# Sums for x of groups 3 to 8 over all 64 features at once, with feature halves exchanged between partition quarters

## The chip, the cores and the metric

The kernel runs on one core of a Trainium2 chip. The core has five engines that run side by side, each in its own order and tied together by semaphores: PE (TensorE, matrix products into PSUM; PEld is its weight load), DVE (VectorE), ACT (ScalarE), POOL (GpSimd) and SP (SyncE, used here only to issue transfers). The metric is the device time of one execution, in microseconds (us); smaller is better.

## The reference

Two blocks follow one another. The first is an attention with a polynomial sketch in place of the softmax; the second is a feed-forward block with an ELU.

```
q, k, v: (4, 4, 1088, 32) float32        S1, S2: (8, 32)
w_in: (128, 2048)      w_out: (2048, 128)

phi(x) = outer product of (S1 x) and (S2 x), 64 features for each row
kv  = sum over s of phi(k)[s, f] * v[s, d]          (64 x 32 for each batch and head)
z   = sum over s of phi(k)[s, f]
x   = (phi(q) @ kv) / (phi(q) . z + 1e-6)           heads side by side: (4352, 128)
h   = x @ w_in
out = where(h > 0, h, exp(min(h, 0)) - 1) @ w_out   (4352, 128)
```

The sums of the title are `phi(q) @ kv`: for each query row and head, 64 features against a 64 x 32 matrix.

## The kernel before

**Tiling.** The 4352 rows of x are 68 half tiles of 64 rows, made into nine groups of eight (the last has four). The feed-forward block goes through the groups in steps `(g, cp)`, each for one of eight pairs of 128-wide slices of the 2048: `mm1` (first product, line L256), the ELU on ACT and DVE (L827, L829, L835), and two steps later the second product (`mm2`, or for most groups `mm2_seven`, L756, with sums made ahead on POOL). There are 64 steps for groups 0 to 7 and a loop for the last group.

**Where x comes from.** While the steps of earlier groups run, x of later groups is prepared. `extra` is a table written out by hand: `at(n, ...)` puts a piece of work right after `mm1` of step n, `mid` after the first half of its ELU, `late` after the second half. All engines keep the order in which the program emits; nothing is reordered by a scheduler.

For one of the groups 2, 3, 4 (with 5), 6 (with 7) and 8:
- `queries(...)` holds PE's part. `q1` (L544) multiplies the queries by S1, S2 and the z-weighted sketch, for the group that comes next; `q5` (L661) makes the sums of the group at hand. Both write to the same four PSUM banks, two of which are those of the next step's `mm1`.
- `q2_den`, `q2_a`, `q2_half` make `phi(q) / denominator` (tile `qp`): 128 partitions, i.e. four quarters of 32 query rows, with the 64 features along the free axis.
- `q4` (L651) is one DVE transpose in 32x32 blocks: in each quarter of the partitions, 32 features come onto the partitions and 32 query rows onto the free axis, for both halves f of the 64 features one after the other (tile `qpT`).
- `q5` then takes, for each head r and each quarter w, two 32x32 matmuls, one for each feature half f; the second adds onto the first. The 16 of f = 0 come first, then `q1`, then the 16 of f = 1.
- `q5_out` (L672) copies the result to `xg`, the operand of `mm1`.

Step 15 holds the queries call for group 2, step 22 for group 3, 30 for groups 4 and 5, 46 for 6 and 7, 62 for 8. The transposes `q4` stand late in steps 14 (`at`), 20, 27 and 28 (two halves), 37 and 38, and 60.

**The sums of K^T V.** `KT_out(b)` transposes the sums of batch b on DVE (L441), writes them to DRAM (`kvd`, L442) and reads them back into each of the four partition quarters (`kvs`, L445; batch 0 into one quarter only). Groups 2 and 3 use batch 1, groups 4 and 5 batch 2, 6 and 7 batch 3; group 8 has rows of all four.

**Transfers.** Nearly all are issued by SP, in program order: the loads, `kvd` and `kvs`, and the output rows (L804 in `fin_seven_b`, 16 transfers for a group; L861 in `fin1`, 8). Each has one of eight semaphores in turn and waits for the transfer eight before it.

Of the kernel before, what the change touches and what calls it, by code (L numbers as in the profile page):

```python
# [12 lines left out]
F32 = mybir.dt.float32  # L13
# [14 lines left out]
def kernel(  # L28
# [21 lines left out]
    nc = tc.nc  # L50
    B, H, S, D = q.shape
    R = S1.shape[0]
    P = 128
# [10 lines left out]
    const = ctx.enter_context(tc.tile_pool(name="const", bufs=1))  # L64
    work = ctx.enter_context(tc.tile_pool(name="wk", bufs=2))
# [75 lines left out]
    wide = S1.dtype != F32  # L141
# [17 lines left out]
    if wide:  # L159
        raw_2 = const.tile([P, 2, 4 * P, 2], U32, name="raw")  # L160
# [163 lines left out]


    kvS = const.tile([P, H, D], F32, name="kvS")
    kvs = {b: const.tile([P, H, 2, D], F32, name=f"kvs{b}") for b in range(B)}
    dram = ctx.enter_context(tc.tile_pool(name="dram", bufs=1, space=bass.MemoryType.DRAM))
    kvd = {b: dram.tile([P, 2 * D], F32, name=f"kvd{b}")[:] for b in range(B)}
    kv_ps, feats, wzs, kf_ps = {}, {}, {}, []  # L330
# [107 lines left out]
    def KT_out(b):  # L438

        kt = work.tile([P, 2 * D], F32, name="kvt", tag="kvt")  # L440
        nc.vector.transpose(kt[:], kv_ps[b][:, :R * R])  # L441
        nc.sync.dma_start(kvd[b], kt[:])  # L442
        src = kvd[b].rearrange("(h p) x -> p h x", h=H)
        for w in range(4 if b else 1):
            nc.sync.dma_start(kvs[b][32 * w:32 * w + 32].rearrange("p h f d -> p h (f d)"), src)  # L445

    def ZC(b, ps):
        zl = work.tile([P, H * R], F32, name="zl", tag="zl")
        nc.scalar.copy(zl[:], ps[:, R * R:R * R + H * R])
        return zl  # L450
# [30 lines left out]
    abw, ans, qp, qpT, xg, xps = {}, {}, {}, {}, {}, {}  # L481
# [48 lines left out]
    def quarter_of(g, w):  # L530

        n = un[g] // 2
        return (*half_tile(g + n * w // 8, n * w % 8), n)

    def q1(g, ps, o, opened):
        for w in range(4):
            b, t, n = quarter_of(g, w)
            m, qs = 64 * n, qE[:, b:b + 1, :] if g == NQ - 1 and b < 2 else qT[b][:, t:t + n, :]
            qs = qs.rearrange("p t s -> p (t s)")
            if g == 2:  # L540
                m, qs = 2 * m, _ap(qs, [[8 * 64, 2], [1, m]])
            for r in range(4):
                rows = slice(32 * r, 32 * r + 32)
                nc.tensor.matmul(ps[r][32 * w:32 * w + 32, o:o + m], SWs[rows, b].rearrange("p x r -> p (x r)"),  # L544
                                 qs[rows], start=not opened, stop=True, skip_group_check=True,
                                 tile_position=(32 * r, 32 * w))
        abw[g] = ps, o
# [79 lines left out]
            nc.scalar.copy(to[:, w], xp[w][:, :256].rearrange("p (m s) -> p m s", s=P))  # L627


    def heads(g):  # L630
        return 2 if un[g] > 4 else H

    def q2_a(g, i):
        m = heads(g) * un[g]
        p = psum.tile([P, 512], F32, name="qa", tag="aux")
        ans[g, i] = p[:, :m * R].rearrange("p (m r) -> p m r", r=R)
        nc.scalar.copy(p[:, :m * R], ans[g][:, m * i:m * i + m].rearrange("p m r -> p (m r)"))

    def q2_half(g, i):
        m = heads(g) * un[g]  # L640
        r = slice(m * i, m * i + m)
        qp[g, i] = work.tile([P, 4 * H, R, R], F32, name="qp", tag="qp", bufs=2)
        a_, b_ = ans.pop((g, i)) if (g, i) in ans else ans[g][:, r], abw[g][:, r, :R]
        nc.vector.tensor_mul(qp[g, i][:, :m], _ap(a_, list(a_.ap[1:]) + [[0, R]]),
                             _ap(b_, [b_.ap[1], [0, R], b_.ap[2]]))

    def q4(g, i=0):

        m = heads(g) * un[g]
        qpT[g, i] = work.tile([P, 4 * H, 2, 32], F32, name="qpT", tag="qpT", bufs=2)  # L650
        nc.vector.transpose(qpT[g, i][:, :m].rearrange("p m f s -> p (m f s)"),  # L651
                            qp.pop((g, i))[:, :m].rearrange("p m i j -> p (m i j)"))

    def q5(g, ps, f):
        m4 = un[g]
        for r in range(4):
            i, o = divmod(m4 * r, heads(g) * un[g])
            for w in range(4):
                b, t, n = quarter_of(g, w)
                rows = slice(32 * w, 32 * w + 32)  # L660
                nc.tensor.matmul(ps[w][32 * r:32 * r + 32, :64 * n], kvs[b][rows, r, f, :],  # L661
                                 qpT[g, i][rows, o:o + 2 * n, f, :], start=(f == 0), stop=(f == 1),
                                 skip_group_check=True, tile_position=(32 * w, 32 * r))
        xps[g] = ps

    def q5_out(g, i=0):
# [7 lines left out]
    def queries(g5, g1, n):  # L674

        hs[steps[n]] = [psum.tile([P, 512], F32, name="h", tag="h", bufs=4) for c in range(2)]
        ps = hs[steps[n]] + [psum.tile([P, 512], F32, name="qps", tag="aux") for _ in range(2)]
        if g5 is not None:
            q5(g5, ps, 0)
        if g1 is not None:  # L680
            q1(g1, ps, 256 if g5 is not None else 0, g5 is not None)
        if g5 is not None:
            q5(g5, ps, 1)


# [297 lines left out]
    def late(n, f, *a):  # L983
        extra.setdefault((n, 1), []).append((f, *a))
# [10 lines left out]
    late(2, make_SWs)  # L995
    late(3, Z_share, 0)
    late(3, KT_out, 0)
    zls = {}

    def sums_out(b):  # L1000
        zls[b] = ZC(b, kv_ps[b])
        KT_out(b)
# [32 lines left out]
    for n, g, nx in ((12, None, 2), (15, 2, None), (22, 3, 4), (30, 4, 6), (46, 6, 8), (62, 8, None)):  # L1035
        at(n, queries, g, nx, n + 1)
        if g is not None:
            mid(n, q5_out, g)
        if nx == 2:
            at(n, weights7, slice(NP - 2, NP))  # L1040
            at(n, q1_out_two, (0, 1))
            mid(n, q1_out_two, (2, 3))
        elif nx is not None:
            mid(n, q1_out, nx)
        if g is not None and len(units[g]) > 1:
            late(n, q5_out, g, 1)
    late(12, q2_den, 2)
    late(13, q2_half, 2, 0)
    at(14, q4, 2)
    mid(15, q2_den, 3)  # L1050
    late(19, q2_a, 3, 0)
    late(19, q2_half, 3, 0)
    late(20, q4, 3)
    late(22, q2_den, 4)
    for n, g, i in ((25, 4, 0), (26, 4, 1), (32, 6, 0), (35, 6, 1)):
        late(n, q2_a, g, i)
    at(26, q2_half, 4, 0)
    late(26, q2_half, 4, 1)
    late(27, q4, 4, 0)
    late(28, q4, 4, 1)  # L1060
    late(31, q2_den, 6)
# [12 lines left out]
    for n in range(2, N):  # L1074
        g, cp = steps[n]
# [29 lines left out]
        g, cp = before  # L1105
# [10 lines left out]
    g = NQ - 2  # L1116
# [53 lines left out]
```

## Time and profile before

| | us |
|---|---|
| median of 3 runs (lowest, highest) | 262.6 (262.52, 263.65) |
| the profiled execution, in all | 262.6 |
| its span | 260.5 |
| PE busy | 255.0 (98%) |
| DVE busy | 186.8 (72%) |
| ACT busy | 183.2 (70%) |
| POOL busy | 158.9 (61%) |

The profile is one execution. Its span runs from the first to the last instruction; 2.1 us lie around it. A line of the time order gives the start in us from the span's start, the length, the engine, the line of the kernel, the operation, what it writes and reads, and a count when neighbours are merged; "SPq" is an issue on SP's queue. One matmul on float32 makes two records. "64*32" at a matmul is the piece of the array that it uses, rows by columns; "64x288" is rows by columns of the moving operand. Busy times of PE overlap, since matmuls are pipelined, so distances from start to start are the better measure.

### The profile page before, as it was taken

Reading aid. Unit: us, or ns where it says so; the run is one execution under the profiler, and the core shown is the slowest. Engines: PE = TensorE matmul, PEld = TensorE weight load, DVE = VectorE, ACT = ScalarE, POOL = GpSimd, SP = SyncE. Lnnn points to the kernel's source line nnn. Section 1 sums busy time; section 2 is a strip of 40 time slices with the busy share of each in tenths; the row PEclk is TensorE's granted clock in tenths of the full one; section 3 lists DMA queues with packets and bytes.
Section 4 is the critical chain, followed back from the end, with each engine's and each line's share of the span. In section 5 each row is a group of like instructions: output and inputs, shape, how many; then the busy total and the mean of one; then the engine's idle time right before and its main releaser. Section 6 shows DMA issues by size and latency. Waiting matters only on the chain.

```text
span 260.5 us, 9833 instructions
## 1 busy us (share of the span) xinstructions
PE 255.0 (98%) x4187; PEld 158.7 (61%) x4187; DVE 186.8 (72%) x352; ACT 183.2 (70%) x358; POOL 158.9 (61%) x202
## 2 busy tenths in 40 slices
PE   8899999999999999999999999999999999999994
PEld 7652333453346667676666666665666666668994
DVE  6899999999988958997567576743465446674641
ACT  2469878766667577776687777775877777777792
POOL 4420007002279996788678798888588888887410
PEclk9999999999999999999999999999999999999999
DMA  6998089012011210012100200020001100110012
GB/s 172 325 362 223 4 236 263 16 48 67 14 19 28 34 32 13 3 18 36 26 0 4 35 8 3 0 31 12 3 3 29 17 4 0 25 18 3 3 28 38
DMA packets 28507, 14.30 MB, mean 55 GB/s; under 512 B 21392, under 2 KB 26640, under 8 KB 28464
## 3 DMA queue, kind: packets, MB, share of 16 engines
q1 hardware_dynamic: 28032, 13.32, 21.1%
q8 instruction: 33, 0.54, 0.9%
q10 hardware_dynamic: 368, 0.30, 0.3%
q0 software_dynamic: 64, 0.07, 0.1%
q14 instruction: 10, 0.08, 0.1%
HBM read 11.31 MB, written 2.36 MB: 52 GB/s over the span
## 4 chain that ended last, share of the span: by engine, by line
PE 97%; DVE 1%; ACT 0%; issue 0%; DVEq 0%
PE h L256 45%; PE pb L756 17%; PE pa L756 13%; PE o L256 5%; PE pb L732 4%; PE ol L256 3%; PE idle L264 1%; PE kv L432 1%; PE h L661 1%; PE abp L340 1%; PE qps L661 1%; PE h L544 1%; PE qtp L614 1%; DVE qp L602 1%; PE xps L621 0%; PE kfps L362 0%
## 5 line engine op out<-in xcount | busy, mean ns | idle before, releaser
L256 PE MATMUL h<-xg,W 128*32 128x512 f32 (+3 forms) x904 | 130.8, 539 | 0.3 <-ACT xg L627 0.3
L835 DVE SCALAR_TENSOR_TENSOR gg<-e,h 128x512 f32<-128x512 f32 x128 | 86.0, 682 | 53.1 <-ACT e L829 48.7
L827 ACT ACTIVATE e<-h 128x512 f32<-128x512 f32 x128 | 75.5, 590 | 46.4 <-PE h L256 44.5
L829 ACT ACTIVATE e<-e 128x512 f32<-128x512 f32 x128 | 80.9, 632 | 3.8
L717 POOL TENSOR_TENSOR tt<-gg 128x512 f32<-128x512 f32 x50 | 64.2, 1284 | 29.5 <-DVE gg L835 23.7
L256 PEld LDWEIGHTS h<-xg,W 128*32 128x32 f32 (+1 forms) x904 | 43.0, 122 | 42.9 <-issue 34.6
L720 POOL TENSOR_TENSOR tt<-gg,tt 128x256 f32<-128x256 f32 x50 | 36.9, 739 | 3.9
L719 POOL TENSOR_TENSOR tt<-tt,gg 128x256 f32<-128x256 f32 x50 | 36.7, 735 | 3.9
L756 PEld LDWEIGHTS pa<-gg,W 128*64 128x64 f32 (+1 forms) x496 | 23.7, 126 | 22.8 <-issue 22.7
L756 PE MATMUL pa<-gg,W 128*64 128x128 f32 (+1 forms) x496 | 30.6, 274 | 0.0
L756 PE MATMUL pb<-tt,SS 128*64 128x128 f32 (+1 forms) x480 | 29.6, 273 | 0.0
L756 PEld LDWEIGHTS pb<-tt,SS 128*64 128x64 f32 (+1 forms) x480 | 22.8, 126 | 0.0
L756 PE MATMUL pa<-tt,SS 128*32 128x128 f32 (+1 forms) x288 | 21.2, 273 | 0.0
L756 PE MATMUL pb<-tt,W 128*64 128x128 f32 (+1 forms) x256 | 19.9, 273 | 0.0
L756 PE MATMUL pb<-gg,SS 128*64 128x128 f32 (+1 forms) x256 | 19.9, 273 | 0.0
L134 POOL TENSOR_TENSOR raw<-raw,tiny 128x512 f32<-128x512 f32 x1 | 1.0, 1043 | 24.7 <-DVE raw L129 24.7
L256 PE MATMUL o<-gg,W 128*32 128x512 f32 x128 | 15.3, 595 | 0.0
L756 PEld LDWEIGHTS pa<-tt,SS 128*32 128x32 f32 (+1 forms) x288 | 13.7, 124 | 0.0
L756 PEld LDWEIGHTS pb<-tt,W 128*64 128x64 f32 (+1 forms) x256 | 12.8, 125 | 0.0
L756 PEld LDWEIGHTS pb<-gg,SS 128*64 128x64 f32 (+1 forms) x256 | 12.8, 125 | 0.0
L732 PE MATMUL pb<-gg,W 128*32 128x256 f32 x192 | 11.5, 380 | 0.0
L887 DVE SCALAR_TENSOR_TENSOR gg<-e,h 128x256 f32<-128x256 f32 x16 | 6.6, 417 | 6.4 <-PE h L256 3.2
(158 smaller groups left out, 271.3 us busy)
## 6 DMA issues: line engine op xcount, KB each, us to landing
raw<-in_moe_w_in_dram SPq DMA_DIRECT2D x8, 256.0 KB, 6.3
raw<-in_moe_w_out_dram SPq DMA_DIRECT2D x8, 256.0 KB, 6.4
out_dram<-ob SPq DMA_DIRECT2D x112, 16.0 KB, 1.6
hd_k<-in_k_dram SPq DMA_DIRECT2D x3, 544.0 KB, 7.2
hd_q<-in_q_dram SPq DMA_DIRECT2D x3, 544.0 KB, 9.3
v<-in_v_dram SPq DMA_DIRECT2D x4, 288.0 KB, 7.9
v<-in_v_dram SPq DMA_DIRECT2D x4, 256.0 KB, 8.8
kvs<-kvd SPq DMA_DIRECT2D x13, 32.0 KB, 2.7
```

The source lines that it names most:

```text
L256: nc.tensor.matmul(dst[c:c + tile], lhs[:, c:c + tile], rhs, skip_group_check=True, tile_position=(0, c), **kw)
L264: nc.tensor.matmul(idle[c:c + tile, :cols], ones[:, :tile], ones[:, :cols], skip_group_check=True, tile_position=(0, c))
L661: nc.tensor.matmul(ps[w][32 * r:32 * r + 32, :64 * n], kvs[b][rows, r, f, :], qpT[g, i][rows, o:o + 2 * n, f, :], start=(f == 0), stop=(f ...
L717: nc.gpsimd.tensor_tensor(_ap(t[:, 0], [[4 * P, 2], [P, 2], [1, P]]), _ap(gs[g, cp][:, 0, P:], [[4 * P, 2]] + us), _ap(gs[g, cp][:, 0], [[ ...
L719: nc.gpsimd.tensor_tensor(t[:, 1], t[:, 2], b11, op=ADD)
L720: nc.gpsimd.tensor_tensor(t[:, 3], b21, t[:, 1], op=SUB)
L732: nc.tensor.matmul(acc[1][0][r:r + width[0], 256 * hi:256 * hi + 256], lhs[:, w:w + width[0]], gg[:, c, 256 * u:256 * u + 256], start=(cp ...
L756: nc.tensor.matmul(bank[r:r + width[0], P * col:P * col + P], lhs[:, w:w + width[0]], rhs[:, u], start=(first and i in ((0,) if g == 1 els ...
L827: nc.scalar.activation(e, hs[g, cp][c][:, :n], RELU, scale=-1.0)
L829: nc.scalar.activation(e, e, EXP, scale=-1.0)
L835: nc.vector.scalar_tensor_tensor(gs[g, cp][:, c, :n], es[g, cp][:, c, :n], -1.0, hs[g, cp][c][:, :n], op0=ADD, op1=MAX)
L887: nc.vector.scalar_tensor_tensor(gs["last", k // 2][:, k % 2, :2 * P], es["last", k // 2][:, k % 2, :2 * P], -1.0, hs["last", k][:, :2 * P ...
```

## The change

For groups 3 to 8 the sums over 64 features become one matmul in place of two.

- `q4` writes its transpose with the feature half as the outer index (tile `qpF`). Then eight transfers on SP (32 partitions each) bring it into a new layout: partitions 0 to 63 hold all 64 features of quarters 0 and 1, partitions 64 to 127 those of quarters 2 and 3, with the two quarters side by side (index e) on the free axis. The target is one of two `halves`, which lie in the space of the first two raw weight tiles, used at the start only.
- `KT_out` reads the sums into a second form, `kv2` (tiles named `kvp`): the two feature halves in neighbouring quarters, for partitions 0 to 63 and, but for batch 0, 64 to 127. The form of before, `kvs`, is kept for batch 1 alone, which group 2 uses.
- `q5` for these groups issues 16 matmuls of 64x32 instead of 32 of 32x32, all ahead of `q1`. Group 2 stays as it was.
- `q4` of group 3 goes from late in step 20 to late in step 19.

```diff
-    kvs = {b: const.tile([P, H, 2, D], F32, name=f"kvs{b}") for b in range(B)}
+    kvs = {1: const.tile([P, H, 2, D], F32, name="kvs1")}
+    kv2 = {b: const.tile([P, H, D], F32, name=f"kvp{b}") for b in range(B)}
...
-        for w in range(4 if b else 1):
+        for w in range(4 if b == 1 else 0):
             nc.sync.dma_start(kvs[b][32 * w:32 * w + 32].rearrange("p h f d -> p h (f d)"), src)
+        for p in range(2 if b else 1):
+            for f in range(2):
+                r = slice(64 * p + 32 * f, 64 * p + 32 * f + 32)
+                nc.sync.dma_start(kv2[b][r], src[:, :, D * f:D * f + D])
...
+    halves = [raw_2[:, c].bitcast(F32).rearrange("p (e m a) w -> p e m (a w)", e=2, a=16) if wide else
+              const.tile([P, 2, 4 * H, 32], F32, name=f"qpE{c}")[:] for c in range(2)]
...
     def q4(g, i=0):
 
         m = heads(g) * un[g]
-        qpT[g, i] = work.tile([P, 4 * H, 2, 32], F32, name="qpT", tag="qpT", bufs=2)
-        nc.vector.transpose(qpT[g, i][:, :m].rearrange("p m f s -> p (m f s)"),
-                            qp.pop((g, i))[:, :m].rearrange("p m i j -> p (m i j)"))
+        if g == 2:
...
+            return
+        t = work.tile([P, 2, 4 * H, 32], F32, name="qpF", tag="qpT", bufs=2)
+        nc.vector.transpose(t[:, :, :m].rearrange("p f m s -> p m f s"),
+                            qp.pop((g, i))[:, :m].rearrange("p m (f i) j -> p m f (i j)", f=2))
+        to = qpT[g, i] = halves[(i + (g > 3)) % 2]
+        for u in range(0, 4, 2):
+            for f in range(2):
+                for e in range(2):
+                    nc.sync.dma_start(to[32 * (u + f):32 * (u + f) + 32, e, :m], t[32 * (u + e):32 * (u + e) + 32, f, :m])
...
+                u = 64 * (w // 2)
+                nc.tensor.matmul(ps[w][32 * r:32 * r + 32, :64 * n], kv2[b][u:u + 64, r, :],
+                                 qpT[g, i][u:u + 64, w % 2, o:o + 2 * n, :], skip_group_check=True,
+                                 tile_position=(u, 32 * r))
...
-        if g5 is not None:
+        if g5 == 2:
             q5(g5, ps, 1)
...
-    late(20, q4, 3)
+    late(19, q4, 3)
```

More of the change, by code (lines that the diff above doesn't have):

```diff
@@ L649, in q4 @@
         m = heads(g) * un[g]
-        qpT[g, i] = work.tile([P, 4 * H, 2, 32], F32, name="qpT", tag="qpT", bufs=2)
-        nc.vector.transpose(qpT[g, i][:, :m].rearrange("p m f s -> p (m f s)"),
-                            qp.pop((g, i))[:, :m].rearrange("p m i j -> p (m i j)"))
+        if g == 2:
+            qpT[g, i] = work.tile([P, 4 * H, 2, 32], F32, name="qpT", tag="qpT", bufs=2)
+            nc.vector.transpose(qpT[g, i][:, :m].rearrange("p m f s -> p (m f s)"),
+                                qp.pop((g, i))[:, :m].rearrange("p m i j -> p (m i j)"))
+            return
[7 more added lines that the diff above has]
+                    nc.sync.dma_start(to[32 * (u + f):32 * (u + f) + 32, e, :m], t[32 * (u + e):32 * (u + e) + 32, f, :m])
     def q5(g, ps, f):
@@ L660, in q5 @@
                 rows = slice(32 * w, 32 * w + 32)
-                nc.tensor.matmul(ps[w][32 * r:32 * r + 32, :64 * n], kvs[b][rows, r, f, :],
-                                 qpT[g, i][rows, o:o + 2 * n, f, :], start=(f == 0), stop=(f == 1),
-                                 skip_group_check=True, tile_position=(32 * w, 32 * r))
+                if g == 2:
+                    nc.tensor.matmul(ps[w][32 * r:32 * r + 32, :64 * n], kvs[b][rows, r, f, :],
+                                     qpT[g, i][rows, o:o + 2 * n, f, :], start=(f == 0), stop=(f == 1),
+                                     skip_group_check=True, tile_position=(32 * w, 32 * r))
+                    continue
+                u = 64 * (w // 2)
+                nc.tensor.matmul(ps[w][32 * r:32 * r + 32, :64 * n], kv2[b][u:u + 64, r, :],
+                                 qpT[g, i][u:u + 64, w % 2, o:o + 2 * n, :], skip_group_check=True,
+                                 tile_position=(u, 32 * r))
         xps[g] = ps
```

## The prediction

> **What bounds the kernel now.** I read the page's shares and the chain that ended last first. The first line gives busy time, the other two the chain by engine and by line.
>
> ```profile
> PE 255.0 (98%) x4187; PEld 158.7 (61%) x4187; DVE 186.8 (72%) x352; ACT 183.2 (70%) x358; POOL 158.9 (61%) x202
> ...
> PE 97%; DVE 1%; ACT 0%; issue 0%; DVEq 0%
> PE h L256 45%; PE pb L756 17%; PE pa L756 13%; PE o L256 5%; PE pb L732 4%; PE ol L256 3%; PE idle L264 1%; PE kv L432 1%; PE h L661 1%; PE abp L340 1%; PE qps L661 1%; PE h L544 1%; PE qtp L614 1%; DVE qp L602 1%; PE xps L621 0%; PE kfps L362 0%
> ```
>
> PE is the whole path: a microsecond by which PE stands still is a microsecond at the end, and there is no slack that could take it back. The matmuls to be changed (L661) hold 2% of the path, so the gain can be a percent at most. The change also feeds them by transfers, which until now they did not need. So the second view is the order in time of SP's queue, from the middle of the kernel (start, length, what).
>
> ```profile
> 84.14 9.60 SPq L804 DMA_DIRECT2D out_dram<-ob  x16
> 93.87 0.35 SPq L442 DMA_DIRECT2D kvd<-kvt  x1
> 95.37 2.56 SPq L445 DMA_DIRECT2D kvs<-kvd  x4
> 113.11 9.48 SPq L804 DMA_DIRECT2D out_dram<-ob  x16
> 122.69 0.38 SPq L442 DMA_DIRECT2D kvd<-kvt  x1
> 124.19 3.07 SPq L445 DMA_DIRECT2D kvs<-kvd  x4
> ```
>
> One queue issues the output rows of the finished group (16), then the K^T V sums of a batch to DRAM, then, when these have landed, four reads of them. It is in order: what is put behind the reads of batch 2 starts at 97.93 (95.37 + 2.56), what is put behind those of batch 3 at 127.26. Against this stands when PE comes to the matmuls, from the time order of PE for groups 3, 4 and 8:
>
> ```profile
> 97.32 0.30 PE L661 MATMUL h<-qpT,kvs 32*32 32x128 f32 x2
> ...
> 126.31 0.41 PE L661 MATMUL h<-qpT,kvs 32*32 32x256 f32 x2
> ...
> 234.25 0.24 PE L661 MATMUL h<-qpT,kvs 32*32 32x64 f32 x2
> ```
>
> and when DVE transposes their data (time order of DVE: group 3, both halves of 4, then 8):
>
> ```profile
> 93.08 1.24 DVE L651 STREAM_TRANSPOSE qpT<-qp 128x1024 f32<-128x1024 f32 x1
> ...
> 118.49 1.20 DVE L651 STREAM_TRANSPOSE qpT<-qp 128x1024 f32<-128x1024 f32 x1
> ...
> 122.07 1.24 DVE L651 STREAM_TRANSPOSE qpT<-qp 128x1024 f32<-128x1024 f32 x1
> ...
> 230.73 0.70 DVE L651 STREAM_TRANSPOSE qpT<-qp 128x512 f32<-128x512 f32 x1
> ```
>
> Transposed data is ready 3.0, 3.0 and 2.8 us before PE needs it. The queue into which the exchange is put is free only 0.6 us after PE's need for group 3 and 0.9 us after it for group 4.
>
> **The change, part by part.** All times stand against the profiled execution: span 260.5 us, 262.6 us in all (2.1 around it), which is the median of the three runs shown.
>
> *The matmuls.* Groups 3, 4, 6 and 8 each lose 16 of 32 L661 matmuls and become 16 of 64x32. Old stages, from the first L661 to the next other matmul: 97.32 to 98.95 = 1.63, 2.06, 1.74 and 0.78 us; sum 6.21, with the query matmuls of L544 between in the first three. The nearest rows to 64x32 are those of L362: two sets of 8, 288 columns wide.
>
> ```profile
> 75.32 0.72 PE L362 MATMUL kfps<-kT,Sxp 64*32 64x288 f32 x16
> 75.83 0.69 PE L362 MATMUL h<-kT,Sxp 64*32 64x288 f32 x16
> 76.45 0.43 PE L756 MATMUL pa<-gg,W 128*32 128x128 f32 x8
> ```
>
> A set takes 0.51 (75.32 to 75.83), with the change of tile shape behind it 0.62, so a change is about 0.12. At 256 columns a set is 0.45, two are 0.90. L544 alone, with its changes, took 0.65 for 256 columns (59.71 to 60.36 in the chain); in group 6 it is narrower, by 2.06 - 1.74, so 0.33. Group 4: 0.90 + 0.13 + 0.65 = 1.68; group 6: 1.36. For groups 3 and 8 (128 and 64 columns) a set is 0.23 and 0.11 if it scales with columns; but halves of 32x32 stages went 0.65, 0.50, 0.39 at 256, 128, 64 columns, and by these ratios it is 0.35 and 0.27. New sum 4.64 to 5.19: a gain of 1.0 to 1.6 us. I take 1.3; for the range 0.6 to 1.6, since the matmuls get some eight more semaphore waits a stage (0.05 us each in the trace).
>
> The Trainium skill (TensorEngine Tiling (Array Packing), Key Properties) says that a change of tiling mode drains the array, which speaks against putting 64x32 between 128x32 and 32x32. The rows' 0.12 are that drain; three more make 0.4 us, already in the sums above, and by the rule without a price I would have had to call the gain open.
>
> *The transposes.* Still seven on DVE, the same elements; L280's, with split patterns, need 1.24 ns an element column (1.35 for 1088) against 1.21 here, so nothing to speak of. Group 3's moves a step forward, to about 90.7, before the gg of 91.39. That gg is then 0.8 us late, is followed by a DVE gap of 0.4 and a place now empty at 93.08, and PE needs its buffer at 95.67. Free; without these gaps it would be 1.2 us. The move also gains nothing: SP reaches the group's transfers at 97.9 either way.
>
> *K^T V reads.* Batch 1 gets four reads more, batch 0 one more: SP is then busy to about 68, with the next issue at 75.26. The first four feed group 2 at 70.75 as before. Batches 2 and 3 keep four reads, half as long. Free.
>
> *The exchange.* 48 transfers, eight for each transpose, 64 KB each (32 KB in group 8), all on SP in program order. Three prices are needed. Issue: transfers of 32 long rows are not in the trace; the 128-row loads took 0.33 to 0.38 us, kvd 0.35, out rows 0.43 with 0.05 between, and now and then one of 1.3 to 1.7, so that 16 took 7.45 to 9.6 (0.47 to 0.6 each). I take 0.45 from start to start, ends 0.37 and 0.6. Landing: kvd (32 KB) landed 1.5 us after its issue, out rows 1.6, kvs 2.7 in the median; I take 2.0, ends 1.5 and 2.7. Start: behind the four reads, 97.95 and 127.3; if the halved reads issue in 0.37 each, 96.9 and 125.7.
>
> - Group 3: 97.95 + 7 x 0.45 + 2.0 = 103.1 against 97.3: PE waits 5.8 us. Ends: 96.9 + 2.6 + 1.5 = 101.0 (3.7), 97.95 + 4.2 + 2.7 = 104.9 (7.5).
> - Group 4, two halves, 16 transfers: 127.3 + 15 x 0.45 + 2.0 = 136.05 against 126.3 is 9.7; the first half's matmuls run meanwhile (0.5): 9.2. Ends 6.0 and 12.2.
> - Group 6: transposes end at 154.8 and 158.0, the output rows before it are out by 150.1, and PE comes at 180.4. Sixteen transfers fit (about 9 us). Free.
> - Group 8: SP's output rows end at 230.5, the transpose at 231.43: 231.45 + 7 x 0.45 + 1.9 = 236.5 against 234.25: 2.25. Ends 1.2 and 4.1.
>
> The query matmuls, mm2 of two steps before and the next mm1 stand behind the waiting matmul in PE's order. ACT and DVE finish the step at hand and then wait as well; nothing can be done ahead. So the three waits, 17.25 us, go to the end whole, and each shifts SP's later positions along with PE's.
>
> *The clock.* PE never stands for more than 1 us in this trace. The only matmuls that follow a standing PE are the opening ones (all of one line, 128x128):
>
> ```profile
> 0.78 3.65 PE L264 MATMUL idle<-const-float32-1.0 128*128 128x256 f32 x8 [0.78 <-PEq L1155]
> ...
> 11.55 0.60 PE L264 MATMUL idle<-const-float32-1.0 128*128 128x256 f32 x2
> ```
>
> At the start 1984 columns (two records have 224) took 3.65 us, later 512 took 0.52 (to 12.07): 1.84 against 1.02 ns a column, a loss of 1.6 us, although the granted clock is shown as 1.00. I count 1.6 for each of the two waits over 5 us and none for the short one: 3.2, ends 0 and 4.8.
>
> The Trainium skill (TensorE: Matmul & The Clock Gate, Part 1: The HAM clock gate) states that after an idle window of some 3.4 us the array goes to half clock until it was busy for another. By that rule, the same two waits would cost 1.7 each (my estimate from it), so 3.4 in place of 3.2 and 282.0 in all; by the granted clock's 1.00, no loss and 278.6.
>
> Sum: 260.5 - 1.3 + 5.8 + 9.2 + 2.25 + 3.2 = 279.65; with 2.1 around it 281.8 us, 7% slower.
>
> **Rivals.**
> - *The transfers are hidden, faster.* If issuing cost next to nothing, the exchange of group 3 would land at 95.4 + 1.5 = 96.9, that of group 4 at 125.7, both ahead of PE: 262.6 - 1.3 = 261.3. The point that decides: twelve issues within 0.4 us. No issue in this trace is under 0.31. Chance 0.03.
> - *Hidden, and the matmuls no cheaper:* if drains and added waits cost the 1.3 us that fewer matmuls bring, 262.6. Needs the same impossible queue. 0.03.
> - *The transfers get in each other's way.* Eight of 64 KB in flight land like the weight loads (256 KB, 6.3 us), not like kvd: 4 us more for each of three waits, 294. For it: source and target are 32 partitions only. Against: DMA stood at 0 to 2 tenths busy there. 0.07.
> - *My forecast:* three waits, 0.87. All low ends: 260.5 - 1.6 + 3.7 + 6.0 + 1.2 + 2.1 = 271.9. All high ends: 260.5 - 0.6 + 7.5 + 12.2 + 4.1 + 4.8 + 2.1 = 290.6.
>
> **How the numbers follow.** 281.8 is the sum. The range 272 to 291 holds the forecast's ends, nine tenths of 0.87, and leaves the rivals out. A measurement of this kernel tells about 0.5% (1.3 us) from no change. Faster is the first rival, held to the edge of that: 0.03; same 0.03; slower 0.94.
>
> **What would show it.** In the changed profile, PE's waits should name the exchange's transfers, with about 6, 9 and 2 us at groups 3, 4 and 8 and none at 6; the first L661-like matmul of group 3 near 103; eight exchange issues on SP directly behind the reads of K^T V, about 3.2 us long; the four 64x32 stages 1.0 to 1.6 us shorter in sum once the wait is over; slow matmuls for some 3 us after the long waits. I am wrong if 32-row issues cost much less than any row here, if PE's matmuls can pass the waiting one, or if landing grows with eight in flight.

## The result and the profile after

The changed kernel takes 291.2 us (median of 4 runs, 290.89 to 292.53) against 262.56 for the kernel before, run beside it on the same chip: 1.109 times the time, 95% interval 1.104 to 1.114. The forecast of 281.8 us had the sign and the mechanism, but is 9.4 us short, and the range ended at 291.0, just below (two of the four executions, 290.89 and 290.93, lie inside it). The profiled execution took 292.53 us in all, its span is 290.8 us, so 30.3 us are to be found between the two spans.

First the page: busy times, the rows of PE and of its granted clock in 40 slices, and the chain by engine.

```profile
PE 269.7 (93%) x4059; PEld 164.3 (57%) x4059; DVE 187.0 (64%) x352; ACT 183.2 (63%) x358; POOL 158.9 (55%) x202
...
PE   8899999999999489996599999999999999968994
...
PEclk9999999999999859999658999999999999997999
...
PE 74%; SPq 12%; DMA 5%; DVE 3%; issue 2%; ACT 2%; DVEq 0%
```

PE has three holes: one at group 3, one at group 4 and a small one at group 8. The chain, which was 97% PE, now holds SP's queue and DMA with 17%. The granted clock has dips of its own, each beginning in a hole or, at group 8, 0.5 us behind it, and lasting past it. PE's busy time rose by 14.7 us although it has less to multiply; I put that down to the matmuls that ran at the low clock and to those that stood half issued in a wait.

Next the order in time of SP's queue (start, length, what).

```profile
95.95 1.73 SPq L450 DMA_DIRECT2D kvp<-kvd  x4
97.78 5.04 SPq L670 DMA_DIRECT2D raw<-qpF  x8
...
133.80 1.73 SPq L450 DMA_DIRECT2D kvp<-kvd  x4
135.63 11.32 SPq L670 DMA_DIRECT2D raw<-qpF  x16
...
256.13 5.51 SPq L670 DMA_DIRECT2D raw<-qpF  x8
```

The exchange stands directly behind the reads of K^T V and begins at 97.78, where 97.95 was forecast. But eight issues take 5.04 us and sixteen 11.32, so one is 0.63 us or more from start to start, not 0.45; the sixteen also hold one issue of 1.89 us, and the eight of group 8 one of 1.13. On PE (time order) the matmuls then wait as each transfer lands:

```profile
96.61 0.65 PE L256 MATMUL h<-xg,W 128*32 128x512 f32 x4
101.18 1.21 PE L685 MATMUL h<-raw,kvp 64*32 64x128 f32 x4 [3.92 <-DMA raw<-qpF]
103.75 1.00 PE L685 MATMUL qps<-raw,kvp 64*32 64x128 f32 x3 [1.36 <-DMA raw<-qpF]
...
134.57 1.08 PE L256 MATMUL h<-xg,W 128*32 128x512 f32 x8
138.99 1.17 PE L685 MATMUL h<-raw,kvp 64*32 64x256 f32 x4 [3.34 <-DMA raw<-qpF]
...
147.81 1.06 PE L685 MATMUL qps<-raw,kvp 64*32 64x256 f32 x2 [0.55 <-DMA raw<-qpF]
...
257.07 1.89 PE L256 MATMUL h<-xg,W 128*64 128x512 f32 x8
...
262.35 0.30 PE L685 MATMUL qps<-raw,kvp 64*32 64x64 f32 x2 [1.60 <-DMA raw<-qpF]
```

From the end of the last matmul before to the last datum: group 3 from 97.26 (96.61 + 0.65) to 104.35, 7.1 us; group 4 from 135.65 to 148.35, 12.7 us, in which the first half's matmuls run; group 8 from 258.96 to 262.93, 4.0 us. Group 6 has no wait on transfers.

Last, the windows around group 3, and the four in which the clock changes at groups 4 and 8 (columns: us, busy time and count of PE, PEld, DVE, ACT, POOL, then the granted clock, the busy share of DMA, GB/s).

```profile
96.00:98.00 2.00, 1.26 (x12) 0.17 (x4) 0.54 (x2) 1.23 (x2) 1.92 (x3) 1.00 0.15 23
98.00:100.00 2.00, 0.00 (x0) 0.00 (x0) 0.50 (x1) 0.00 (x0) 1.65 (x3) 0.91 0.34 74
100.00:102.00 2.00, 0.82 (x4) 0.36 (x4) 0.00 (x0) 0.00 (x0) 0.00 (x0) 0.50 0.44 99
...
104.00:106.00 2.00, 1.99 (x57) 1.15 (x58) 0.00 (x0) 0.00 (x0) 0.00 (x0) 0.50 0.03 8
106.00:108.00 2.00, 2.00 (x60) 1.22 (x32) 0.97 (x3) 1.27 (x5) 0.00 (x0) 0.50 0.00 0
108.00:110.00 2.00, 2.00 (x40) 1.74 (x36) 1.74 (x5) 0.83 (x3) 0.47 (x1) 0.53 0.03 8
110.00:112.00 2.00, 2.00 (x36) 0.87 (x32) 1.93 (x4) 1.09 (x2) 1.84 (x3) 1.00 0.00 0
...
140.00:142.00 2.00, 0.73 (x3) 0.18 (x2) 0.00 (x0) 0.00 (x0) 0.00 (x0) 0.65 0.47 109
...
154.00:156.00 2.00, 2.00 (x15) 0.91 (x14) 0.07 (x1) 0.58 (x1) 1.71 (x2) 0.94 0.00 0
...
262.00:264.00 2.00, 1.36 (x36) 1.11 (x38) 0.00 (x0) 0.50 (x5) 0.00 (x0) 0.87 0.07 16
...
266.00:268.00 2.00, 2.00 (x14) 0.95 (x12) 0.00 (x0) 0.32 (x1) 1.90 (x2) 0.78 0.00 0
```

PE stops at 97.3; the clock falls to 0.50 a good 2 us later. The last data lands at 104.35, PE is full from there, and the clock stays at 0.50 until about 109.9. That is 5.5 us at half clock, some 2.8 us of work lost. The same reading gives 5.9 us at half clock after group 4's wait (2.95 lost) and 3.4 after group 8's (1.7 lost): 7.5 us in all.

These rows also give the times at which the clock changes, since it is either 1.00 or 0.50: down at 99.63, 140.59 and 263.47, up again at 109.87, 154.24 and 266.88 us. The distances between neighbours in time are 10.24, 30.72, 13.65, 109.23 and 3.41 us: 3, 9, 4, 32 and 1 times 3.413. In the traces of the other runs they are whole multiples of it too, from a start that differs from run to run. Whether the clock falls, and how long it stays down, thus depends on where a wait lies on that grid. Before each fall PE was busy for 1.04, 1.17 and 1.21 us of the last 3.41; a stretch of the grid with 1.89 and one with 2.48 us left the clock up. It rose after stretches that were busy throughout.

The balance, from matching products on both sides: the first steady product behind group 3's sums is 9.3 us later than before, behind group 4's 24.4, unchanged from there until group 6 adds 0.2; behind group 8's it is 30.0, and so at the last matmul (the span's other 0.3 us lie in the landing of the last output rows). Waits of 23.8 and a clock of 7.5 make 31.3; the other 1.3 are the matmuls saved and the half of group 4's that ran inside its wait.

### The profile page after: what moved, and what is told of

It is laid out like the page before. It is cut to its first block, busy times and chain, and to the rows that moved or that the text cites. A ratio compares the mean times of both kernels' runs of the same rounds, so it can differ in the third digit from the quotient of the medians.

```text
span 290.8 us, 9673 instructions
## 1 busy us (share of the span) xinstructions
PE 269.7 (93%) x4059; PEld 164.3 (57%) x4059; DVE 187.0 (64%) x352; ACT 183.2 (63%) x358; POOL 158.9 (55%) x202
## 4 chain that ended last, share of the span: by engine, by line
PE 74%; SPq 12%; DMA 5%; DVE 3%; issue 2%; ACT 2%; DVEq 0%
PE h L256 33%; PE pb L780 13%; PE pa L780 10%; SPq L670 6%; SPq L828 5%; PE o L256 5%; PE pb L756 4%; PE ol L256 2%; DMA raw<-qpF 2%; PE qps L685 1%; DMA hd_k<-in_k_dram 1%; DMA kvd<-kvt 1%; SPq L450 1%; PE h L685 1%; PE h L549 1%
## 5 line engine op out<-in xcount | busy, mean ns | idle before, releaser
L780 PEld LDWEIGHTS pa<-gg,W 128*64 128x64 f32 (+1 forms) x496 | 24.3, 129 | 23.6 <-issue 23.4
L780 PE MATMUL pa<-gg,W 128*64 128x128 f32 (+1 forms) x496 | 31.8, 283 | 0.0
L780 PE MATMUL pb<-tt,SS 128*64 128x128 f32 (+1 forms) x480 | 30.9, 282 | 0.0
L780 PEld LDWEIGHTS pb<-tt,SS 128*64 128x64 f32 (+1 forms) x480 | 23.8, 132 | 0.1
L780 PE MATMUL pa<-tt,SS 128*32 128x128 f32 (+1 forms) x288 | 21.8, 281 | 0.0
L696 ACT COPY xg<-h 128x128 f32<-128x128 f32 (+2 forms) x10 | 2.5, 301 | 30.7 <-PE qps L549 26.1
L685 PE MATMUL h<-raw,kvp 64*32 64x256 f32 (+2 forms) x64 | 11.9, 394 | 9.9 <-DMA raw<-qpF 9.9
L780 PE MATMUL pb<-gg,SS 128*64 128x128 f32 (+1 forms) x256 | 20.6, 282 | 0.0
L572 DVE STREAM_TRANSPOSE abw<-h 128x256 f32<-128x256 f32 (+1 forms) x6 | 2.1, 369 | 24.9 <-ACT xg L696 24.9
L685 PE MATMUL qps<-raw,kvp 64*32 64x256 f32 (+2 forms) x64 | 9.3, 412 | 5.1 <-DMA raw<-qpF 5.1
```

What stands on the lines that cost most here:

```text
L685: nc.tensor.matmul(ps[w][32 * r:32 * r + 32, :64 * n], kv2[b][u:u + 64, r, :], qpT[g, i][u:u + 64, w % 2, o:o + 2 * n, :], skip_group_chec ...
L780: nc.tensor.matmul(bank[r:r + width[0], P * col:P * col + P], lhs[:, w:w + width[0]], rhs[:, u], start=(first and i in ((0,) if g == 1 els ...
```

## The experiments

All kernels below are the changed kernel with the edit shown. Times are medians, with the kernel before beside them on the same chip.

**The matmuls without the exchange.** The forecast gave the matmuls alone 1.3 us; a rival gave them nothing.

```diff
-        to = qpT[g, i] = halves[(i + (g > 3)) % 2]
-        for u in range(0, 4, 2):
...
+        qpT[g, i] = t
```

> The changed kernel without the exchange: the 48 transfers are left out and q5 reads the transposed tile where DVE left it, with the same 16 matmuls of 64x32 per stage (the sums of groups 3 to 8 are therefore of mixed-up features). Everything else stays. Theory: the loss is the waits for the exchange and the clock that falls in them, and nothing else; the matmuls themselves save nothing, since the undisturbed stage of group 6 went from 1.74 to 1.99 us. Then 262.5 to 263.6 us, granted clock 1.00 throughout. Rival A (the prediction's term): fewer matmuls save 1.0 to 1.6 us, so 261.0 to 261.6. Rival B: the added reads of K^T V, the moved transpose or the split transposes cost something too: over 264.

Measured: 261.39 us against 262.42, ratio 0.9957 (0.9944 to 0.9969). All three holes and all dips of the clock are gone. The four stages last 1.41, 1.84, 1.52 and 0.43 us, 5.20 in sum against 6.21 before. So the matmuls are worth 1.0 us (not nothing, as was expected here), the lower end of the 1.0 to 1.6 worked out, and the whole rest of the loss, some 30 us, hangs on the exchange. The time orders of PE at group 6, without the exchange

```profile
180.00 0.40 PE L681 MATMUL h<-qpF,kvp 64*32 64x256 f32 x1
...
181.07 0.24 PE L549 MATMUL h<-qE,SWs 32*32 32x64 f32 x2
...
181.52 0.66 PE L776 MATMUL pa<-gg,W 128*64 128x128 f32 x8
```

and with it (the changed kernel)

```profile
204.83 0.40 PE L685 MATMUL h<-raw,kvp 64*32 64x256 f32 x1
...
206.49 0.24 PE L549 MATMUL h<-qE,SWs 32*32 32x64 f32 x2
...
206.82 0.66 PE L780 MATMUL pa<-gg,W 128*64 128x128 f32 x8
```

show that the exchange costs there too, where its data had landed long before: the sums take 1.66 us with it and 1.07 without, the whole stage 1.99 against 1.52 (1.74 before the change). I put the difference down to matmuls that check for the landing of sixteen transfers, though that is inferred and not tried by itself. It is no fixed price for each transfer: with eight of them (the run with half the transfers, below) the same sums take 1.08 us and the stage 1.61. In undisturbed group 6 the change therefore saves nothing and costs 0.25 us.

**Another order of these matmuls.** The same without the exchange, the two quarters of different partition halves taken in turn (`w2`, `w2 + 2`), so that neighbours in the order use different rows of the array.

```diff
+            for w2 in range(2):
+                for r in range(4):
+                    i, o = divmod(m4 * r, heads(g) * un[g])
+                    for w in (w2, w2 + 2):
```

> As the run without the exchange (sums of groups 3 to 8 again of mixed-up features), and the 16 matmuls in another order: quarters 0 and 2 of all four heads first, then quarters 1 and 3. In the changed kernel quarters 0 and 1 follow each other on the same piece of the array; here eight different pieces come before one is used again, as in the rows of L362 from which the prediction took its price. Theory: this order is what the price lacked; the stage of group 6 falls from 1.99 to about 1.4 us and the whole by 1.0 to 2.0 us against the run without the exchange. Rival: the stage is bound by the columns that run through the two halves of the array's rows, whatever the order: the same time within 0.3 us.

Measured: 260.95 us against 262.42, ratio 0.9944 (0.9931 to 0.9956); stages 1.29, 1.72, 1.41 and 0.38, 4.80 in sum. The order brings 0.4 us, less than the theory and more than the rival said.

**Half the transfers.** DVE transposes a second time straight into the target. Two of four blocks then need no move, and four transfers are left of eight.

```diff
+        src = qp.pop((g, i))[:, :m].rearrange("p m (f i) j -> p m f (i j)", f=2)
+        nc.vector.transpose(t[:, :, :m].rearrange("p f m s -> p m f s"), src)
+        nc.vector.transpose(to[:, :, :m].rearrange("p f m s -> p m f s"), src)
...
-                for e in range(2):
+                e = 1 - f
```

> The changed kernel with four transfers a transpose in place of eight: the four that only move a block within its own partitions are replaced by a second DVE transpose that writes straight to the target (1.24 us of DVE each). Theory (issues in one queue set the waits, 0.63 us each): group 3 waits 4.5 us instead of 7.1, group 4 about 7 to 8 instead of 12.9, group 8 about 2 instead of 4.1 and keeps its clock: 279 us, 277 to 282. Rival (landing or a common delay before the first transfer sets them): the first data come as late as before and the rest with them, 287 to 291.

Measured: 278.32 us (276.88 to 278.89), ratio 1.0593 (1.0560 to 1.0627). The time order of SP:

```profile
97.86 2.51 SPq L671 DMA_DIRECT2D raw<-qpF  x4
...
133.41 5.80 SPq L671 DMA_DIRECT2D raw<-qpF  x8
...
246.26 2.41 SPq L671 DMA_DIRECT2D raw<-qpF  x4
```

Same start, same 0.63 us each, half the number: 12.9 us of the 28.6 lost are back. The added transposes on DVE (5 us more of busy time) did not delay the start. The gain is more than the issues that were saved (2.5, 5.5 and 3.1 us), and group 4's and group 8's waits, now shorter, left the granted clock at 1.00; group 3's still let it fall.

**The price of the low clock.** Matmuls on the weights are put into the waits, ahead of the sums that stand there and between the halves of group 4 (into a PSUM bank that is overwritten afterwards), so that PE never stands.

```diff
+        if g5 in (3, 4, 8):
+            fill(ps[0], {3: 28, 4: 26, 8: 14}[g5])
```

> The changed kernel with matmuls on weights ahead of the waiting ones, into columns that the sums then overwrite: 28 rounds of four 128x32 with 256 columns before group 3, 26 before group 4 and 18 half rounds between its halves, 14 before group 8. The transfers and their order are untouched. Theory: about 7.6 us of the loss is work done at half clock after the waits (104.35 to 109.9, 148.35 to 154.6, 263.4 to 266.9 us), so with PE kept busy the granted clock stays 1.00 and the time is 283 to 285.5. Rival (the clock costs no more than the 3.2 us of the prediction, or the waits themselves are longer than read): 287.5 to 289; no effect: 291.

Measured: 300.42 us, ratio 1.1442 (1.1427 to 1.1458). It says nothing on the price, because the filling was too long. The chain in order of time (start, length, what):

```profile
97.38 12.09 PE h L703 x224
```

A round took 0.43 us, twice what I had counted, so filling ran until 109.5 although the last transfer was issued by 104.6 and lands some 2 us later. It shows only that the clock stays at 1.00 in all stages when PE is kept at work. With half the rounds (14, 14 and 8, and 9 half rounds between the halves of group 4):

```diff
+            if g == 4 and r == 2:
+                fill(ps[0], 9, (64, 96))
...
+            fill(ps[0], {3: 14, 4: 14, 8: 8}[g5])
```

> The run with filling matmuls again, sized by what a round took there (0.43 us and not half of it, so that they ran 37 us in sum against waits of 24): 14 rounds before group 3, 14 before group 4 and 9 half rounds between its halves, 8 before group 8, which is 6.0, 6.0, 3.9 and 3.4 us. Theory: granted clock 1.00 throughout, and the 7.6 us of work lost at half clock come back: 283 to 285.5. Rival (the fall of the clock costs what the prediction gave it, 3.2 us): 287 to 289.

Measured: 287.3 us (286.48 to 290.09), ratio 1.0931 (1.0907 to 1.0955). Below the changed kernel by 3.9 us, where 6 to 8 were expected, and inside the 287 to 289 of the rival. The profiled execution is the longest of the four (290.09); the other three took 286.48 to 287.88 with a mean granted clock of 1.00. In the profiled one the clock is 1.00 at groups 4 and 8. At group 3 the filling ended early (time order of PE, then windows with the clock third from last):

```profile
96.89 6.27 PE L703 MATMUL h<-W 128*32 128x256 f32 x112
...
105.55 0.38 PE L687 MATMUL qps<-raw,kvp 64*32 64x128 f32 x2 [1.85 <-DMA raw<-qpF]
```

```profile
106.00:107.00 1.00, 1.00 (x56) 0.59 (x42) 0.00 (x0) 0.00 (x0) 0.00 (x0) 0.76 0.00 0
107.00:108.00 1.00, 1.00 (x31) 0.38 (x12) 0.12 (x1) 0.42 (x3) 0.00 (x0) 0.50 0.00 0
...
150.00:151.00 1.00, 1.00 (x18) 0.40 (x22) 0.00 (x0) 0.00 (x0) 0.00 (x0) 1.00 0.00 0
```

A gap of 1.85 us was enough there for the clock to fall, and it did so after PE was busy again: at 106.52, one stretch of 3.413 us before it rose, and in the stretch ahead of the fall (103.11 to 106.52) PE was busy for 1.56 us. From the last datum to the next steady product, group 4 took 9.2 us in the changed kernel and 6.9 here, group 8 6.9 and 5.2, group 3 8.7 and 7.9. These differences make 4.8 us; the reading of the windows says 7.5. Between them stands group 3, where the clock fell here as well (3.4 us at half clock, 1.7 lost), which makes 6.5. In time, the three executions with an unbroken clock are only 3.3 to 4.7 us faster than the changed kernel's median, but here the queue ran later (the exchange of group 3 began at 98.48, 0.7 us later). By the rows the low clock thus cost more than the 3.2 us forecast, between 4.8 and 7.5; the times alone do not show that much, and the runs do not settle it further.

**An earlier start.** The output rows of groups 1 and 2 are issued behind the exchange (late in steps 22 and 30) rather than before it.

```diff
+    late(22, rows_out, 1)
+    late(30, rows_out, 2)
```

> The changed kernel with the output rows of groups 1 and 2 issued late in steps 22 and 30, behind the exchange and not ahead of it; nothing else. Theory (what stands ahead on SP's queue sets the start): group 3's exchange starts at about 93.2 instead of 97.8 and PE waits 2.5 us instead of 7.1; group 4's starts about 5.5 us earlier against PE and PE waits about 7.4 instead of 12.9; group 8 as before: 278 to 281 us. Rival (the exchange is late by its own length or by DVE's transposes, whatever stands ahead of it): 289 to 292.

Measured: 285.59 us (284.52 to 285.72), ratio 1.0867 (1.0848 to 1.0886). SP's order:

```profile
89.92 0.34 SPq L443 DMA_DIRECT2D kvd<-kvt  x1
93.16 1.73 SPq L450 DMA_DIRECT2D kvp<-kvd  x4
94.99 5.04 SPq L670 DMA_DIRECT2D raw<-qpF  x8
...
128.92 10.76 SPq L670 DMA_DIRECT2D raw<-qpF  x16
```

It lies between theory and rival. The exchange starts 2.8 us earlier at group 3, less than the 4.1 by which `kvd` does, since here the reads had to wait 3.2 us for its landing rather than 1.9; its length is unchanged, and group 4's sixteen issues end at 139.7 against a PE that comes at 131.9. Place in the queue is worth 5.6 us, number is worth 12.9.

**All of it together.** Four transfers, the other matmul order, output rows later, the queries of groups 3 and 4 one step later, and group 8's preparation seven to eight steps earlier.

```diff
-    for n, g, nx in ((12, None, 2), (15, 2, None), (22, 3, 4), (30, 4, 6), (46, 6, 8), (62, 8, None)):
+    for n, g, nx in ((12, None, 2), (15, 2, None), (23, 3, 4), (31, 4, 6), (46, 6, 8), (62, 8, None)):
...
-    late(60, q4, 8)
+    late(53, q4, 8)
```

> All of it together, to see whether the gain of the matmuls can be had: four transfers a transpose with the second DVE transpose, the alternating order of the matmuls, the output rows of groups 1 and 2 behind the exchange, the queries calls of groups 3 and 4 one step later (23 and 31), and group 8's preparation eight steps earlier. Theory: exchange of group 3 landed by about 98 against a PE that comes at about 100.5, that of group 4 by about 129 against 129.6, group 8 long before: no wait, granted clock 1.00, and the matmuls' 1.4 us less some 0.2 to 0.5 of added semaphore waits a stage: 261 to 262.5. Rival (a wait is left at group 4, or the later queries delay the first product of group 4): 263 to 267.

Measured: 262.24 us (262.01 to 262.88) against 262.58, ratio 0.9994 (0.9985 to 1.0002), clock 1.00. The 30 us are gone, and so is most of the gain: the stages are 1.70, 2.18, 1.46 and 0.40. At group 4 PE is still held up (time order of its weight loads):

```profile
130.65 0.10 PEld L682 LDWEIGHTS qps<-raw,kvp 64*32 64x32 f32 x1 [0.35 <-DMA raw<-qpF]
```

So a last step: the reads of K^T V of batches 2 and 3, whose data is needed no sooner than the exchange's, also go behind the exchange.

```diff
+    late(22, KT_read, 2)
+    late(23, rows_out, 1)
+    late(30, KT_read, 3)
+    late(31, rows_out, 2)
```

> The run with everything together (262.24 us), and the reads of the sums of K^T V of batches 2 and 3 issued late in steps 22 and 30, behind the exchange. There the last matmuls of groups 3 and 4 still stood some 0.4 us for transfers that landed at about 101.5 and 130.6 us. Theory: group 3's exchange starts at about 93.5 instead of 95.3 and group 4's at 121.3 instead of 123.4, nothing waits, the stages of groups 3 and 4 fall from 1.70 and 2.18 us to 1.3 to 1.4 and 1.75 to 1.9: 261.2 to 261.8, which is faster than before. Rival (the longer stages there come from the added semaphore checks and not from late transfers): 262.2 again.

Measured: 261.77 us (261.55 to 261.88) against 262.42, ratio 0.9971 (0.9960 to 0.9983): faster than both kernels, by 0.7 us. SP and PE, in time order:

```profile
93.04 2.52 SPq L675 DMA_DIRECT2D raw<-qpF  x4
...
120.84 6.78 SPq L675 DMA_DIRECT2D raw<-qpF  x8
```

```profile
129.70 0.40 PE L686 MATMUL h<-raw,kvp 64*32 64x256 f32 x1
...
131.50 0.66 PE L791 MATMUL pa<-gg,W 128*64 128x128 f32 x8
```

The last issue of group 4 is out at 127.6, PE comes at 129.70, and its stage is 1.80 us where the version before it had 2.18. Compared with the same order without any exchange (260.95), 0.8 us are still lost; part of that is group 3's stage, which stayed at 1.70 where 1.3 to 1.4 was expected: the profile puts the wait before its second half down to DVE and not to a transfer.

**The moved transpose.** Group 3's transpose goes back to step 20, as before the change.

```diff
-    late(19, q4, 3)
+    late(20, q4, 3)
```

> The changed kernel with group 3's transpose back late in step 20; nothing else. Theory (SP's queue reaches the exchange at 97.8 us whatever DVE does at 91 or 93): the same as the changed kernel, 290.5 to 292. Rival (the transpose is part of the wait): 2 to 3 us more, 293 to 294.5.

Measured: 291.94 us (290.68 to 292.98), ratio 1.1103 (1.1066 to 1.1139), as with the move.

```profile
96.31 1.73 SPq L450 DMA_DIRECT2D kvp<-kvd  x4
98.14 5.04 SPq L670 DMA_DIRECT2D raw<-qpF  x8
```

The exchange still begins right behind the reads of K^T V. The step earlier brings nothing, because the queue has not come that far.

**What makes an issue 0.6 us?** First, a quarter of the bytes in the same 48 transfers (the rest of the exchanged data is left out); then as many transfers of 128 rows instead of 32, each a quarter as wide.

```diff
-                    nc.sync.dma_start(to[32 * (u + f):32 * (u + f) + 32, e, :m], t[32 * (u + e):32 * (u + e) + 32, f, :m])
+                    nc.sync.dma_start(to[32 * (u + f):32 * (u + f) + 32, e, :m // 4], t[32 * (u + e):32 * (u + e) + 32, f, :m // 4])
```

> To find what sets the price of an issue, which the prediction had at 0.45 us and the trace at 0.63: the changed kernel with each exchange transfer cut to a quarter of its row (512 B instead of 2 KB, 256 B in group 8; three quarters of the exchanged data are left out). Price by bytes: 0.35 to 0.45 us from start to start. Price by transfer and its shape of 32 rows: 0.58 to 0.65 as before, and about 290 us, less what the shorter landing saves (under 1 us a wait).

```diff
+        for k in range(4):
+            for e in range(2):
+                c = slice(m // 4 * k, m // 4 * k + m // 4)
+                nc.sync.dma_start(to[:, e, c], t[:, 1 - e, c])
```

> The changed kernel with the same number of exchange transfers and the same bytes, but each of 128 rows of 512 B in place of 32 rows of 2 KB (256 B rows in group 8), from and to the same partitions, so that no block changes its quarter (the sums of groups 3 to 8 are of mixed-up features). If the 32-row shape is what costs, an issue falls to the 0.31 to 0.38 us plus 0.05 of the 128-row rows in the trace of before, and the waits of groups 3, 4 and 8 shrink by about 1.6, 3.3 and 1.6 us, to 282 to 286 us in all; if any transfer from partitions to partitions costs so much, 0.58 to 0.65 and about 290.

Measured, one execution each: 290.45 and 291.01 us. The groups of these issues (ns: least, median, most; then first and last start) in the changed kernel, with a quarter of the bytes, and with all rows:

```profile
L670 SPq DMA_DIRECT2D raw<-qpF x48: 512/582/1887, 97.8 to 261.1; - x48
```

```profile
L670 SPq DMA_DIRECT2D raw<-qpF x48: 512/582/1413, 98.6 to 259.1; - x48
```

```profile
L670 SPq DMA_DIRECT2D raw<-qpF x48: 470/592/1724, 97.9 to 260.0; - x48
```

Neither bytes nor the 32-row shape set the price; the median stays at 0.58 to 0.59 us. In the changed kernel's profile the issues that have DRAM on one side keep the lower price:

```profile
L828 SPq DMA_DIRECT2D out_dram<-ob x112: 315/430/1810, 84.0 to 285.1; - x112
L450 SPq DMA_DIRECT2D kvp<-kvd x14: 303/430/1604, 60.2 to 135.1; - x14
```

What these three forms of the exchange have in common, and the rows of the forecast did not, is that they go from one place of the core's own memory to another. That this is the cause is likely, but it was not separated from all else.

## Why the prediction was right and where it failed

**Right: three waits, their order and places.** PE waits on the transfers at groups 3, 4 and 8, not at 6. The two long exchanges stand directly behind the reads of K^T V (begin 97.78 for a forecast 97.95). Nothing is done ahead of a waiting matmul and all of it goes to the end. Without the transfers the loss is gone.

**Right: the parts costed at nothing.** The reads of K^T V, the transposes on DVE, and the moved transpose of group 3: with it or without, 291.2 and 291.9 us.

**Failed: the step "I take 0.45 from start to start, ends 0.37 and 0.6".** It is 0.63, past the upper end. The row I took it from was of output rows to DRAM; the change's transfers are of another kind, for which the trace of before had no row, and the bounds should have been open upwards. Seven gaps, fifteen and seven, by 0.18 us each, are 5.2 us, and the two long issues at groups 4 and 8 (1.89 and 1.13 us) add 1.9. Against that, group 4's exchange began as PE came (135.63 and 135.65), not 1.0 us later as forecast. The landing, 2.0 us, was as taken. The waits, forecast 5.8, 9.2 and 2.25, measured 7.1, 12.3 (12.7 less the 0.45 of a half's matmuls) and 4.0: 6.1 us more, each near its upper end or at it.

**Failed: the clock, "1.6 for each of the two waits over 5 us and none for the short one".** By the windows it is 2.8, 2.95 and 1.7, in sum 7.5 for a forecast 3.2; by the rows of the filled waits 4.8 to 6.5, by their times 3.3 to 4.7. Two errors lie in it. The opening matmuls of the trace, from which 1.6 came, were a poor row for a stall in mid-kernel: the clock's records of that trace begin only at 5.99 us, so the 1.00 shown for these matmuls measures nothing. And the short wait of group 8 was counted as free, where the clock was down for 3.4 us behind it. The Trainium skill (TensorE: Matmul & The Clock Gate, Part 1: The HAM clock gate) says half clock after an idle window of some 3.4 us, until busy for another, and that these windows run on freely, whatever the kernel does. The stretches of 3.413 us found above agree. After a wait the clock stayed down to the end of the first stretch that was busy throughout: 3.4 us of full work at group 8, 5.5 and 5.9 at groups 3 and 4. But a stretch need not be idle throughout, as 1.56 us of work in it did not prevent a fall. Where a wait lies on that grid is luck, and with it part of the 7.5 us.

**Mis-sized: the matmuls.** The forecast took 1.3 of 1.0 to 1.6, without the exchange it is 1.0; with it, group 6's stage grew by 0.25 and brought nothing. "Some eight more semaphore waits a stage (0.05 us each in the trace)" does not describe it: with eight transfers group 6's sums took as long as with none (1.08 and 1.07 us), with sixteen 0.6 us longer.

The terms together: waits 6.1 and clock 4.3 above the forecast make 10.4 of the 10.7 us between the sum of 281.8 and the profiled execution's 292.5.

**The rivals.** "Hidden, faster" needed twelve issues within 0.4 us and did not come. But its time, 261.3, is what the matmuls alone do (261.39), and a kernel whose exchange is nearly hidden reaches 261.77, by fewer transfers and a better place in the queue and not by a cheaper issue. "Hidden, and the matmuls no cheaper" fell with the first, and without the exchange the matmuls are cheaper by 1.0. "The transfers get in each other's way" did not come either: landing was 2.0 us in the median, and a quarter of the bytes changed nothing. But at 0.63 us for an issue only some three are in flight at a time, so eight at once were not tried.

## What to carry to other kernels

Before a change that puts transfers in front of a saturated engine, count issues rather than bytes: here the number of transfers was worth 12.9 us, their place in the queue 5.6, their bytes nothing, and the matmuls they served 1.0. Where the trace has no row for the very kind of transfer (from and to the same memories), leave the price open upwards. And add to each wait of some microseconds on TensorE the time at half clock behind it, here 1.7 to 3 us of work for each by the clock's rows, or keep PE at work in it, as the filling did (a few matmuls were not enough).

## What the runs showed of the hardware that was not expected

- An issue on SP for a transfer within the core's memory took 0.58 us in the median (0.63 from start to start), whether of 16 or 64 KB, on 32 or 128 partitions; with DRAM on one side 0.43.
- The granted clock changed only at whole multiples of 3.413 us from one another, in every trace here. It fell to 0.50 some 2.4 us after PE stopped at group 3, 4.9 and 4.5 us after it at groups 4 and 8, where a few matmuls broke the wait, and once behind a gap of only 1.85 us (after 6.3 us of filling). It did so after stretches of 3.41 us with 1.04 to 1.56 us of work, not after those with 1.89 and 2.48, and stayed down for 3.4 to 5.9 us of full work. With four transfers the waits of groups 4 and 8 left it at 1.00.
- A stage whose data had landed long before was still 0.5 us longer when it was fed by sixteen transfers (1.99 against 1.52 us); fed by eight it was 0.1 longer (1.61).
